# Top-k attention, a maxout MoE and a routed MoE: the planner also orders the transfers and gives out buffers as it places steps

## The chip, the cores and the metric

The kernel runs on one core of one Trainium2 chip. The metric is device time in microseconds from the first to the last instruction, as the median of several runs. TensorE (PE) multiplies, VectorE (DVE) does the top-k, ScalarE (ACT) copies out of PSUM and takes exponentials, GpSimd (POOL) does elementwise work between SBUF tiles, and SyncE (SP) issues the transfers.

## The reference, cut to what matters

```python
# q, k, v: (4 batches, 8 heads, 576 tokens, 64)
scores = q @ k.T / sqrt(64)
kth    = 32nd largest score of each row          # top_k = 32
attn   = softmax(where(scores >= kth, scores, -1e9))
x      = attn @ v                                # as (2304 tokens, 512)
h      = max(x @ w1, x @ w2, x @ w3)             # 512 x 768 each
x      = h @ w_out                               # 768 x 512
logits = x @ w_gate + modality_bias[modality_id] # 8 experts
e      = argmax(logits);  g = softmax(logits)[e]
out    = g * (relu(x @ e_w1[e]) @ e_w2[e])       # 512 x 1024, 1024 x 512
```

The weights of the first MoE come as 64-bit floats and are decoded on the chip. Products are made from a high and a low part of each operand (three matmuls instead of one).

## The kernel before, in words

The attention is cut into 72 units. A `full` unit is one query tile of 128 rows and one pair of heads; a `comb` unit joins the 64 rows that are left of a batch for two pairs. For each unit: `q_load` and `q_split` fetch a query tile and split it in high and low parts, `q_prep` transposes it; `scores` writes the scores to the PSUM tile `s` (one buffer, four banks, two key halves: half 1 first, then half 0), and `s_copy` copies each half to the SBUF tile `ss` (four buffers). Two folds on VectorE (L785) form the larger and the smaller of the two halves; a fold reads half 0 from PSUM and half 1 from `ss`. Eight rounds of `max` and `match_replace` on the folded rows give the threshold. Then `mask` and `expo` make the softmax numerators, `pt` transposes them, `av` multiplies by the values (PSUM tile `m`, two buffers), and `norm` and `x_split` write the input of the first MoE. Keys are loaded, split and transposed per pair of heads (`k_load`, `k_split`, `k_prep`), values per pair (`v_load`); `v_max` reads the values once more for a scale.

Three groups of query tiles per batch go through the first MoE (`moe1_steps`: three matmul chains per 128 columns, evacuated by ScalarE and VectorE, then `w_out`, transposes and gate). Its weights are decoded in 24 pieces during the first units (`weight_steps`). `route_early` computes the routing of the first three batches near unit 67: sums, ranks, and a table (L1416, TensorE, into a tile `m`). The last MoE groups run after the attention (`tail`), and then the experts.

The program names the steps slot by slot (one slot per unit, with positions between 0 and 1 inside it). `Plan.add` records for each step its engine, an estimated length, and the buffers that it reads and writes as (name, tenant, part, number of buffers). `Plan.run` then places steps by list scheduling: on the engine that is free first, the ready step with the smallest urgency, which is its number less the `soon` of the function that issued it (table `SOON`). A step waits for `data` (the end of other steps, plus a tail and a wake-up time) and for `order` (the other step has been placed). In `add` before, the first user of a tenant of a buffer name gets an `order` edge from the first user of the tenant named just before it, and in `run` every user of a tenant gets `data` edges from all users of the tenant that is as many back as there are buffers. Both follow the order in which the program names the tenants.

`tc.manual_schedule` keeps the order in which `run` calls the steps for PE, ACT, DVE and POOL. SP's queue is ordered by the framework's own scheduler. A transfer has a length of 60 to 540 ns in the plan and lands 2300 ns and a given extra time later.

Of the kernel before, what the change touches and what calls it, by code (L numbers as in the profile page):

```python
# [21 lines left out]
BIG = float(2.0 ** 100)  # L22
UP = float(2.0 ** 16)
# [3 lines left out]
class Plan:  # L27
# [16 lines left out]
    def add(self, engine, length, f, reads=(), writes=(), shared=False, lands=0):  # L44

        soon = self.soon
# [4 lines left out]
        data, order = set(), set()  # L51
        for places, w in ((reads, False), (writes, True)):
            for name, tenant, part, bufs in places:
                all_ = self.held.setdefault(name, {})
                if tenant not in all_:
                    if all_:
                        order.add(next(reversed(all_.values()))[0][0])
                    all_[tenant] = []
                uses = all_[tenant]
                if uses:  # L60
                    order.add(uses[0][0])
                data.update(m for m, q, v in uses if (w or v) and (q == part or q is None or part is None))
                uses.append((n, part, w))
                self.bufs[name] = bufs
        data.discard(n)
        order.discard(n)
        self.steps.append((engine, length, f, shared, data, order, lands, n - soon))

    def run(self):
        steps = self.steps  # L70
        for name, tenants in self.held.items():
            uses = [{n for n, _, _ in u} for u in tenants.values()]
            for old, now in zip(uses, uses[self.bufs[name]:]):
                for n in now:
                    steps[n][4].update(old)
        for n, s in enumerate(steps):
            s[4].discard(n)
            s[5].difference_update(s[4])
        after = [[] for _ in steps]
        left = [len(s[4]) + len(s[5]) for s in steps]  # L80
        for n, s in enumerate(steps):
            for m in s[4]:
                after[m].append((n, True))
            for m in s[5]:
                after[m].append((n, False))
        free = dict.fromkeys(self.WAKE, 0)
# [3 lines left out]
        locked = 0  # L90
        for n, s in enumerate(steps):
            if not left[n]:
                heapq.heappush(come[s[0]], (0, s[7], n))
        while True:
# [21 lines left out]
            end = t + length + self.TAIL[e] + lands  # L116
            for m, data in after[n]:
                to = steps[m][0]
                at = t if not data else t + length if e == to == "PE" else end + self.WAKE[to] + (self.SPARE if e != to else 0)
                ready[m] = max(ready[m], at)  # L120
                left[m] -= 1
                if not left[m]:
                    heapq.heappush(come[to], (ready[m], steps[m][7], m))
            f()
        assert not any(left)
# [4 lines left out]
def moe_chain_kernel(  # L130
# [52 lines left out]
    nc.sync.dma_start(wg, w_gate.rearrange("(c p) e -> p c e", p=128))  # L183
# [67 lines left out]
    nc.sync.dma_start(x2_dram[0:1, :], z)  # L251
# [40 lines left out]
    def whole(redo):  # L292
# [81 lines left out]
        def fetch(src, piece, signs=False):  # L374
# [6 lines left out]
            if wide:  # L381
                raw = rawf[:, k % 4 * 2 * PIECE:(k % 4) * 2 * PIECE + 2 * n * m].bitcast(I32)
                add("SP", 60, lambda: nc.sync.dma_start(raw.rearrange("p (c f) -> p c f", c=n), src.bitcast(I32)), (),
                    [at("raw", k, None, 1, k % 4)], lands=5 * n * m)
# [3 lines left out]
            add("SP", 60, lambda: nc.sync.dma_start(w.rearrange("p (c f) -> p c f", c=n), src), (), [at("wst", k, None, 1, k % 2)],  # L388
                lands=3 * n * m)
# [91 lines left out]

        def setup_bias():
# [7 lines left out]

            def f1():
                mod = box["mod"]
# [1256 lines left out]
```

## Time and profile before

| | |
|---|---|
| median of 3 runs | 1105.55 us (1104.78 to 1107.02) |
| profiled execution | 1103.24 us, span 1101.5 us |
| TensorE matmul | 944.6 us, 86% |
| VectorE | 769.1 us, 70% |
| ScalarE | 702.2 us, 64% |
| GpSimd | 560.6 us, 51% |
| mean granted TensorE clock | 0.929 of full |

Busy time is the time in which an engine executes an instruction; matmuls are pipelined and their ends are modelled. In a list in order of time, the brackets behind an instruction give the idle time of its engine just before it and what ended it. Stretches and starts are in microseconds from the span's start. Line numbers are those of the kernel before.

### The profile page before, as it was taken

To read this page: it belongs to the slowest core of one execution; us is meant where nothing else is said; L and a number is where in the kernel's file an instruction comes from. 1 tells how busy PE (TensorE), PEld (TensorE's weight loads), DVE (VectorE), ACT (ScalarE), POOL (GpSimd) and SP (SyncE) were. 2 spreads that over 40 slices of the span, in tenths; PEclk is the share of its full clock that TensorE was granted. 3 is DMA by queue.
4 is the path that set the end of the run, shared out by engine and by line. 5 is a ranking of instruction groups with operands and counts; after the bars stand their busy time and mean duration, and the time that the engine had idled before them with its cause. 6 is when DMAs were issued, how large, how long until landed. Compare 5 with 4: busy or idle time off the path is not lost. (4 is left out here: it accounts for less than half of the span.)

```text
span 1101.5 us, 22044 instructions
## 1 busy us (share of the span) xinstructions
PE 944.6 (86%) x7518; PEld 777.7 (71%) x7518; DVE 769.1 (70%) x2510; ACT 702.2 (64%) x1624; POOL 560.6 (51%) x831
## 2 busy tenths in 40 slices
PE   1546569999999899999999999974989989989995
PEld 0434448787778788777878778753779868868884
DVE  2799999989997969998887999996353511151110
ACT  1689898898877878887778887762453222342221
POOL 1578787576766666676566776662331111131010
PEclk9857689999999989999989999996989999999998
DMA  4652320224001113001011100000030331142000
GB/s 84 195 144 91 101 83 11 60 53 138 7 6 35 37 42 79 26 5 34 9 48 30 43 9 6 27 1 1 1 120 31 138 103 49 39 155 77 20 30 25
DMA packets 83795, 60.48 MB, mean 55 GB/s; under 512 B 67009, under 2 KB 67009, under 8 KB 83650
## 3 DMA queue, kind: packets, MB, share of 16 engines
q1 hardware_dynamic: 80770, 49.32, 15.8%
q0 software_dynamic: 2880, 9.44, 2.5%
q8 instruction: 65, 1.06, 0.4%
q14 instruction: 80, 0.66, 0.2%
HBM read 49.30 MB, written 9.44 MB: 53 GB/s over the span
## 5 line engine op out<-in xcount | busy, mean ns | idle before, releaser
L792 DVE MAX8 tk<-wk 128x8 f32<-128x288 f32 x576 | 235.9, 445 | 0.0
L847 POOL TENSOR_TENSOR ss<-mk,ss 128x576 f32<-128x576 bf16 x144 | 186.2, 1306 | 54.8 <-ACT mk L845 54.6
L803 DVE MATCH_REPLACE8 wk<-tk,wk 128x288 f32<-128x288 f32 x432 | 188.3, 441 | 0.0
L785 DVE TENSOR_TENSOR wk<-s,ss 128x576 f32<-128x576 f32 x144 | 106.9, 749 | 38.4 <-ACT ss L726 36.9
L845 ACT ACTIVATE mk<-ss,kb 128x576 bf16<-128x576 f32 x144 | 107.7, 773 | 33.7 <-POOL kb L741 33.5
L870 PE MATMUL t<-ident,ss 128*128 128x128 f32 x576 | 93.2, 297 | 34.2 <-ACT ss L853 31.5
L726 ACT ACTIVATE ss<-s 128x576 f32<-128x576 f32 x144 | 88.3, 647 | 50.6 <-PE s L715 49.1
L853 ACT ACTIVATE ss<-ss,kb 128x576 f32<-128x576 f32 x144 | 112.3, 782 | 6.4 <-POOL ss L847 6.1
L917 POOL TENSOR_SCALAR ss<-ss,r,nil 128x576 f32<-128x576 f32 x116 | 95.4, 828 | 30.5 <-DVE r L907 27.1
L1601 ACT ACTIVATE hid<-ph 128x512 f32<-128x512 f32 x36 | 21.5, 598 | 137.8 <-PE ph L1600 137.8
L715 PE MATMUL s<-ks,qt 128*128 128x288 f32 x512 | 96.1, 337 | 12.2 <-DVE wk L785 7.1
L870 PEld LDWEIGHTS t<-ident,ss 128*128 128x128 f32 x576 | 68.8, 151 | 47.3 <-ACT ss L853 37.1
L1625 POOL DMA_INDIRECT out_dram<-bo,tab x18 | 18.3, 1017 | 155.7 <-ACT bo L1624 148.4
L715 PEld LDWEIGHTS s<-ks,qt 128*128 128x128 f32 x512 | 80.9, 215 | 19.1 <-DVE wk L785 8.1
L1589 DVE TENSOR_TENSOR bxl<-px,bxh 128x512 fp32r<-128x512 f32 x18 | 12.4, 690 | 113.0 <-ACTq L1637 96.6
L874 ACT ACTIVATE pt<-t 128x512 f32<-128x512 f32 x144 | 84.3, 601 | 1.6 <-PE t L870 1.5
L938 PE MATMUL m<-pt,v 128*64 128x128 f32 x1024 | 75.7, 294 | 0.0
L938 PEld LDWEIGHTS m<-pt,v 128*64 128x64 f32 x1024 | 59.4, 145 | 11.9 <-issue 11.9
L1059 DVE SCALAR_TENSOR_TENSOR hb<-m,wfac,hb 128x320 f32<-128x320 f32 (+2 forms) x96 | 47.1, 491 | 19.5 <-PE m L1050 18.2
L1070 POOL TENSOR_TENSOR hl<-hb,hh 128x320 f16<-128x320 f32 (+2 forms) x54 | 36.9, 683 | 45.0 <-ACT hh L1065 44.9
L1600 PE MATMUL ph<-e1h,bxh 128*128 128x512 f32 x144 | 58.8, 408 | 1.2 <-ACT bxh L1588 0.7
L1621 PE MATMUL py<-e2h,bhh 128*128 128x512 f32 x144 | 58.0, 403 | 1.4 <-ACT bhh L1612 1.4
(312 smaller groups left out, 2734.3 us busy)
## 6 DMA issues: line engine op xcount, KB each, us to landing
raw<-in_moe_w_dram SPq DMA_DIRECT2D x6, 2048.0 KB, 9.7
raw<-in_moe_w_dram SPq DMA_DIRECT2D x18, 512.0 KB, 3.8
kraw<-in_v_dram SPq DMA_DIRECT2D x16, 288.0 KB, 2.8
kraw<-in_k_dram SPq DMA_DIRECT2D x32, 128.0 KB, 2.5
qraw<-in_q_dram SPq DMA_DIRECT2D x64, 64.0 KB, 1.9
v<-in_v_dram SPq DMA_DIRECT2D x32, 128.0 KB, 2.4
x_rows<-row SPq DMA_DIRECT2D x16, 256.0 KB, 2.0
raw<-in_moe_w_out_dram SPq DMA_DIRECT2D x6, 512.0 KB, 3.5
```

The lines of the kernel that those rows point to most:

```text
L715: PE.matmul(ST[u][:, hf, t, :HALF], qt[:, i, :], KS[bat(u), p][:, hd, k0:k0 + HALF], start=(n == 0), stop=(n == len(parts) - 1))
L726: A.activation(SS[u][:, :, hf * HALF:(hf + 1) * HALF], ST[u][:, hf, :, :HALF], AF.Copy)
L785: V.tensor_tensor(WK[u][:, :, w, :], ST[u][:, 0, :, :HALF], SS[u][:, :, HALF:S], op=op)
L792: V.max(TK[u][:, t, r * 8:r * 8 + 8], WK[u][:, t, 0, :])
L803: add("DVE", 426, lambda: V.match_replace(WK[u][:, t, 0, :], TK[u][:, t, r * 8:r * 8 + 8], WK[u][:, t, 0, :], NEG), [tk_at(u, (t, r))], [w ...
L845: A.activation(box["m"], SS[u][:, t, :], AF.Relu, bias=KTH[u][:, t, 1:2], scale=-BIG)
L847: add("POOL", 1250, lambda: G.tensor_tensor(SS[u][:, t, :], box["m"], SS[u][:, t, :], op=OP.subtract), [M], rows_at(u, t))
L853: A.activation(SS[u][:, t, :], SS[u][:, t, :], AF.Exp, bias=KTH[u][:, t, 0:1], scale=-scale * UP, accum_out=SUM[u][:, t:t + 1])
L870: PE.transpose(t[:, c, :], SS[u][:, i, c0:c0 + 128], ident)
L874: A.activation(o, box["t"], AF.Copy)
L917: add("POOL", 790, lambda: G.tensor_scalar(SS[u][:, t, :], SS[u][:, t, :], RR[u][:, t:t + 1], nil, op0=OP.mult, op1=OP.add), [at("r", u, N ...
L938: PE.matmul(ps[hd * 64:(hd + 1) * 64, 0, :], vt[:, c, hd, :], PT[u, hd][:, c, :], start=False, stop=(c == KC - 1), skip_group_check=True)
```

## The change

`Plan.add` no longer chains the tenants of a buffer in program order: it notes which step opens a tenant. `Plan.run` checks, when it is about to place such a step, which tenant had taken the buffer that comes free next. If that one has steps to come, the step is put aside until they are placed; if it ends later than now, the step comes back at that time; otherwise it takes the buffer. The order of the tenants is thus the order of placing.

SP is added to the engines whose order is kept. Each transfer is a step of its own, of 570 ns, that ends 2000 ns later plus its bytes at 180 per ns, with transfers in flight sharing that rate. The key, value and modality loads are split into single transfers; the gate weights and a zero row move from the head of the kernel to slot 2 (`late_loads`), the weight scales from slot -6 to -2. `k_prep` takes its buffer with the transposes instead of with the first copy. `s_copy` of half 0 moves from the slot before the unit's folds to position 0.13 of the unit's own slot, behind both folds, and the folds name both halves of `ss` as read. The table `SOON` is new. The diff, cut to its core:

```diff
-    TAIL = {"PE": 165, "ACT": 112, "DVE": 85, "POOL": 45, "SP": 2300}
-
-    SPARE = 0
+    TAIL = {"PE": 165, "ACT": 112, "DVE": 85, "POOL": 45, "SP": 2000}
+    RATE = 180.0
...
-    def add(self, engine, length, f, reads=(), writes=(), shared=False, lands=0):
...
-        data, order = set(), set()
+        data, order, opens, uses_ = set(), set(), [], []
         for places, w in ((reads, False), (writes, True)):
             for name, tenant, part, bufs in places:
-                all_ = self.held.setdefault(name, {})
-                if tenant not in all_:
-                    if all_:
-                        order.add(next(reversed(all_.values()))[0][0])
-                    all_[tenant] = []
-                uses = all_[tenant]
-                if uses:
+                uses = self.held.setdefault((name, tenant), [])
+                if not uses:
+                    opens.append((name, tenant))
+                elif uses[0][0] != n:
                     order.add(uses[0][0])
                 data.update(m for m, q, v in uses if (w or v) and (q == part or q is None or part is None))
                 uses.append((n, part, w))
+                if (name, tenant) not in uses_:
+                    uses_.append((name, tenant))
                 self.bufs[name] = bufs
         data.discard(n)
-        order.discard(n)
-        self.steps.append((engine, length, f, shared, data, order, lands, n - soon))
+        self.steps.append((engine, length, f, shared, data, order - data, size, n - self.soon, opens, uses_))
...
-        for name, tenants in self.held.items():
-            uses = [{n for n, _, _ in u} for u in tenants.values()]
-            for old, now in zip(uses, uses[self.bufs[name]:]):
-                for n in now:
-                    steps[n][4].update(old)
+        after, left, todo = [[] for _ in steps], [], {}
...
-            e = best[1]
+            now, e = best
             n = heapq.heappop(here[e])[1] if here[e] else heapq.heappop(come[e])[2]
-            _, length, f, shared, _, _, lands, _ = steps[n]
-            t = max(free[e], ready[n])
+            _, length, f, shared, _, _, size, _, opens, uses = steps[n]
+            late = 0
+            for x in opens:
+                had = taken.setdefault(x[0], [])
+                if len(had) >= self.bufs[x[0]]:
+                    old = had[-self.bufs[x[0]]]
+                    if todo[old]:
+                        wait.setdefault(old, []).append(n)
+                        late = None
+                        break
+                    late = max(late, max(t if d == e == "PE" else t + self.TAIL[d] + self.WAKE[e] for t, d in ends[old]))
+            if late is None:
+                continue
+            if late > now:
+                push(n, late)
+                continue
+            for x in opens:
+                taken[x[0]].append(x)
+            t = max(free[e], ready[n], now)
...
-            end = t + length + self.TAIL[e] + lands
+            end = t + length + self.TAIL[e]
+            if e == "SP":
+                end = max(end, pipe) + size / self.RATE
+                pipe = max(pipe, t + 1500) + size / self.RATE
...
+        def late_loads():
+            add("SP", ISSUE, lambda: nc.sync.dma_start(wg, w_gate.rearrange("(c p) e -> p c e", p=128)), (), [at("wg", 0)])
+            add("SP", ISSUE, lambda: nc.sync.dma_start(x2_dram[0:1, :], z), (), [at("rows", 0, "zero")])
...
+            m32 = modality.bitcast(I32).rearrange("(t two) -> t two", two=2)
+            for b in range(B):
+                add("SP", ISSUE, lambda b=b: nc.sync.dma_start(
+                    box["mod"][:, b, 1:NTT], m32[b * S:b * S + KC * 128, 0:1].rearrange("(c p) o -> p (c o)", p=128)),
+                    (), [at("bias", 0, b)], size=2048)
+                add("SP", ISSUE, lambda b=b: nc.sync.dma_start(box["mod"][:TL, b, 0:1], m32[b * S + KC * 128:(b + 1) * S, 0:1]),
+                    (), [at("bias", 0, b)], size=2048)
...
         def k_load(b, p):
-            def f():
-                raw = ap_.tile([128, NTT, 2, D], F32, name="kraw", bufs=2)
...
-            add("PE", 168, f, [at("kx", (b, p), (1, i)) for i in range(2)], [t])
+            add("PE", 168, f, [at("kx", (b, p), (1, i)) for i in range(2)], [t, ks_at(b, p, ("room", 2))])
...
         def v_load(b, p):
-            def f():
...
-                VT[b, p] = vt
-            add("SP", 300, f, (), [at("v", (b, p), None, 5)], lands=2000)
+            for i, hd in ((0, 0), (0, 1), (1, 0), (1, 1), (2, 1)):
+                def f(i=i, hd=hd):
+                    if (b, p) not in VT:
+                        VT[b, p] = ap_.tile([128, NTT, 2, D], F32, name="v", bufs=5)
+                    vt, src = VT[b, p], of_batch(v, b)[2 * p + hd]
...
+                add("SP", ISSUE, f, (), [at("v", (b, p), (i, hd), 5)], size=(131072, 16384, 16384)[i])
...
-                add("DVE", 664, f, [at("s", u, 0), ss_at(u, 0, 1), ss_at(u, 1, 1)], [wk_at(t, w) for t in range(2)])
+                add("DVE", 664, f, [at("s", u, 0)] + [ss_at(u, t, hf) for t in range(2) for hf in range(2)],
+                    [wk_at(t, w) for t in range(2)])
...
+        WSCALE = -2
         EARLY = 67
-        SOON = {"scores": 120, "s_copy": 120, "q_split": 120, "q_prep": 120, "k_split": 120, "k_prep": 120, "mm": -60, "ev": -30}
+        SOON = {"q_prep": 180, "prefetch_first": 180, "k_prep": 135, "k_split": 125, "scores": 120, "s_copy": 90,
+                "q_split": 90, "x_split": 55, "setup_bias": 45, "pt": 45, "f": 25, "av": 20, "recip": -5, "setup_routing": -5,
+                "k_load": -5, "mask": -5, "first_expert": -15, "v_max": -20, "norm": -25, "ev": -30, "weight_scales": -55,
+                "g": -60, "route_early": -70, "mm": -75, "scale_rows": -95, "v_load": -115}
...
-                sched(-6, weight_scales)
+                sched(WSCALE, weight_scales)
+                sched(2, late_loads)
...
+                if u0 is not None:
+                    put(0.13, s_copy, u0, 0)
...
                     put(0.36, scores, un, 0)
-                    put(0.42, s_copy, un, 0)
...
-            add("SP", 300, lambda: nc.sync.dma_start(raw1, e_w1[ds(e_value(first_e), 1)].rearrange("o (c p) f -> p (o c) f", p=128)),
-                [at("first", 0)], [at("raw", "first", None, 1, i) for i in range(4)], lands=12000)
+            add("SP", ISSUE, lambda: nc.sync.dma_start(raw1, e_w1[ds(e_value(first_e), 1)].rearrange("o (c p) f -> p (o c) f", p=128)),
+                [at("first", 0)], [at("raw", "first", None, 1, i) for i in range(4)], size=2097152)
...
-            with tc.manual_schedule(engines={E.PE, E.Activation, E.DVE, E.Pool}):
+            with tc.manual_schedule(engines={E.PE, E.Activation, E.DVE, E.Pool, E.SP}):
```

## Rows read from the trace of the kernel before

**Rows 1.** Busy time of an engine over the span (busy us, share, instructions), from the page.
```profile
PE 944.6 (86%) x7518; PEld 777.7 (71%) x7518; DVE 769.1 (70%) x2510; ACT 702.2 (64%) x1624; POOL 560.6 (51%) x831
```
**Rows 2.** Busy time by stage: stretch, length, busy us (instructions) per engine, PEclk, DMA, GB/s.
```profile
0.00:12.00 12.00, 0.75 (x4) 0.56 (x4) 3.96 (x17) 2.32 (x4) 3.13 (x14) 1.00 0.49 94
12.00:38.30 26.30, 7.03 (x35) 5.83 (x35) 7.22 (x37) 6.84 (x23) 3.79 (x8) 1.00 0.54 127
38.30:155.30 117.00, 68.68 (x436) 54.07 (x434) 115.86 (x352) 101.33 (x221) 91.52 (x110) 0.68 0.42 122
175.00:725.00 550.00, 526.54 (x4715) 436.32 (x4712) 495.81 (x1686) 453.08 (x1093) 366.40 (x585) 0.97 0.13 35
736.60:757.70 21.10, 0.58 (x6) 0.44 (x4) 20.23 (x85) 7.43 (x14) 8.51 (x13) 0.61 0.00 0
757.70:802.00 44.30, 43.15 (x376) 31.23 (x375) 13.75 (x47) 18.32 (x46) 11.33 (x18) 0.95 0.01 1
848.00:1101.50 253.50, 230.10 (x1113) 188.19 (x1113) 62.09 (x158) 69.86 (x125) 39.37 (x37) 0.97 0.21 71
```
**Rows 3.** SP in order of time: start us, us, engine, line, operation, out<-in, count.
```profile
0.76 0.46 SPq L183 DMA_DIRECT2D wg<-in_moe_w_gate_dram  x1
...
10.33 0.47 SPq L594 DMA_DIRECT2D v<-in_v_dram  x1
...
29.89 0.59 SPq L596 DMA_DIRECT2D v<-in_v_dram  x1
30.59 0.53 SPq L633 DMA_DIRECT2D qraw<-in_q_dram  x1
```
**Rows 4.** ScalarE in order of time, at the start; idle time and releaser in brackets.
```profile
13.23 0.81 ACT L547 ACTIVATE kx<-kraw 128x512 fp32r<-128x512 f32 x2
...
32.74 0.42 ACT L647 ACTIVATE qx<-qraw 128x256 fp32r<-128x256 f32 x1 [18.21 <-DMA qraw<-in_q_dram]
33.06 1.07 ACT L573 ACTIVATE ks<-t 128x512 fp32r<-128x512 f32 x2
```
**Rows 5.** TensorE in order of time, at the start.
```profile
14.66 1.26 PE L568 MATMUL t<-identr,kx 128*128 128x128 f32 x8 [0.15 <-DVE kx L551]
```
**Rows 6.** VectorE in order of time: the first fold.
```profile
38.28 0.76 DVE L785 TENSOR_TENSOR wk<-s,ss 128x576 f32<-128x576 f32 x1
```
**Rows 7.** TensorE in order of time, near the end of the attention.
```profile
736.58 0.60 PE L870 MATMUL t<-ident,ss 128*128 128x128 f32 x4
757.74 0.55 PE L1416 MATMUL m<-rhs,sel 128*128 128x15 bf16 x15 [20.57 <-DVE rhs L1411]
758.14 0.43 PE L1050 MATMUL m<-xh,w3h 128*128 128x320 f16 x1
...
761.43 0.56 PE L934 MATMUL m<-pt,v 64*64 64x128 f32 x4
```
**Rows 8.** VectorE in order of time: first folds of the last two units.
```profile
738.00 0.76 DVE L785 TENSOR_TENSOR wk<-s,ss 128x576 f32<-128x576 f32 x1 [0.51 <-ACT ss L726]
...
769.13 1.42 DVE L785 TENSOR_TENSOR wk<-s,ss 128x576 f32<-128x576 f32 x2 [1.65 <-ACT ss L726]
```
**Rows 9.** All engines in order of time: a second fold, the next scores, the next fold.
```profile
282.65 0.75 DVE L785 TENSOR_TENSOR wk<-s,ss 128x576 f32<-128x576 f32 x1
...
283.54 1.30 PE L715 MATMUL s<-ks,qt 128*128 128x288 f32 x8
...
290.81 0.75 DVE L785 TENSOR_TENSOR wk<-s,ss 128x576 f32<-128x576 f32 x1
```
**Rows 10.** Groups by line: busy us, mean ns; idle us before them, releasers.
```profile
L845 ACT ACTIVATE mk<-ss,kb 128x576 bf16<-128x576 f32 x144 | 107.7, 773 | 33.7 <-POOL kb L741 33.5
...
L726 ACT ACTIVATE ss<-s 128x576 f32<-128x576 f32 x144 | 88.3, 647 | 50.6 <-PE s L715 49.1 <-DVE wk L785 1.3
```
**Rows 11.** Transfers by line: count, KB each, median us from issue to landing.
```profile
kraw<-in_k_dram SPq DMA_DIRECT2D x32, 128.0 KB, 2.5
...
v<-in_v_dram SPq DMA_DIRECT2D x32, 128.0 KB, 2.4
```

More of the change, by code (lines that the diff above doesn't have):

```diff
@@ L22 @@
 BIG = float(2.0 ** 100)
+ISSUE = 570
 UP = float(2.0 ** 16)
@@ L42, in clear, with add @@
         self.steps, self.held, self.bufs = [], {}, {}
-    def add(self, engine, length, f, reads=(), writes=(), shared=False, lands=0):
-        soon = self.soon
+    def add(self, engine, length, f, reads=(), writes=(), shared=False, size=0):
         if not self.live:
@@ L89, in run, with push @@
         ready = [0] * len(steps)
-        locked = 0
-        for n, s in enumerate(steps):
+        taken, ends, wait = {}, {}, {}
+        locked, pipe, out = 0, 0, 0
+        def push(n, t):
+            heapq.heappush(come[steps[n][0]], (t, steps[n][7], n))
+        for n in range(len(steps)):
             if not left[n]:
-                heapq.heappush(come[s[0]], (0, s[7], n))
+                push(n, 0)
         while True:
@@ L115, in run @@
             free[e] = t + length
-            end = t + length + self.TAIL[e] + lands
+            end = t + length + self.TAIL[e]
+            if e == "SP":
+                end = max(end, pipe) + size / self.RATE
+                pipe = max(pipe, t + 1500) + size / self.RATE
+            f()
+            out += 1
             for m, data in after[n]:
                 to = steps[m][0]
-                at = t if not data else t + length if e == to == "PE" else end + self.WAKE[to] + (self.SPARE if e != to else 0)
+                at = t if not data else t + length if e == to == "PE" else end + self.WAKE[to]
                 ready[m] = max(ready[m], at)
@@ L122, in run @@
                 if not left[m]:
-                    heapq.heappush(come[to], (ready[m], steps[m][7], m))
-            f()
-        assert not any(left)
+                    push(m, ready[m])
+            for x in uses:
+                todo[x] -= 1
+                ends.setdefault(x, []).append((end - self.TAIL[e], e))
+                if not todo[x]:
+                    for m in wait.pop(x, ()):
+                        push(m, ready[m])
+        assert out == len(steps)
         self.clear()
@@ L565, in f @@
                     kx = KX2[b, p]
+                    if (b, p) not in KS:
+                        KS[b, p] = ap_.tile([128, 2, TL + S], F32R, name="ks", bufs=4)
                     box[hd] = psT.tile([128, 512], F32, name="t").bitcast(F32R)
@@ L570, in g @@
                 def g(hd=hd):
-                    if hd == 0:
-                        KS[b, p] = ap_.tile([128, 2, TL + S], F32R, name="ks", bufs=4)
                     A.activation(KS[b, p][:, hd, TL:S], box[hd], AF.Copy)
-                add("PE", 344, f, [at("kx", (b, p), (0, i)) for i in range(2)], [t])
+                add("PE", 344, f, [at("kx", (b, p), (0, i)) for i in range(2)], [t, ks_at(b, p, ("room", hd))])
                 add("ACT", 477, g, [t], [ks_at(b, p, hd)])
```

67 lines of the change are left out of this document (31 added, 36 removed).

## The prediction

> **What bounds the kernel now.** I read the busy shares first, then the busy time by stage, then, at the two stages with idle engines, the instructions in order of time. The shares [rows 1] name no single bound: TensorE is busy 86% of the span, VectorE 70%. The stages [rows 2] do. From 38.3 to 155.3 us VectorE is busy 115.86 of 117.00 us: the top-k and the decoding of the weights bound that stage, and TensorE idles in 48 us of it. From 175 to 725 TensorE is busy 526.54 of 550.00 us and VectorE 495.81: TensorE bounds, with VectorE not far behind. From 848 on, TensorE is busy 230.10 of 253.50 us in the experts, which are not planned by the code that changes. So the two long middle stages are full, and an ordering change finds little in them. What is not full are two short stretches: the first 38.3 us, in which VectorE works 3.96 + 7.22 = 11.18 us and idles 27.1, and 736.6 to 757.7, in which TensorE works 0.58 of 21.10 us.
>
> The first hole is one of transfer order. From 10.33 to 30.59 SP issues only values and modality ids: 25 of v and 9 of the ids, 34 issues in 20.26 us, 0.60 us each [rows 3]. The third query load stands behind them. ScalarE has the splitting of that query tile ahead of the copies of the first key tile in its queue, and waits 18.21 us for it, until 32.74; then it copies the keys (33.06), and the first fold of VectorE starts at 38.28 [rows 4, 6]. TensorE had the key transposes ready at 14.66 + 1.26 = 15.9 [rows 5].
>
> The second hole is one of buffer order. TensorE's next instruction at 736.6 is the routing table's matmul (L1416); it waits 20.57 us for VectorE, which is busy with that routing [rows 2, 7]. Right behind it stand matmuls of the first MoE that wait for nothing, and the value products of the last six units, of which the first runs at 761.43 [rows 7]. The old planner gives the two PSUM buffers "m" out in the order in which the program names them: every user of "m" that the program names after the table must wait until the table has had its own. The stall is thus in the plan itself. The last unit's fold comes at 769.13, 31 us after the one before, at 738.00 [rows 8].
>
> **The change, part by part.**
>
> *Transfers as planned steps.* SP joins the engines that keep the planner's order, and each transfer is a step of 570 ns (0.60 us measured) that ends after a latency and its size at 180 bytes per ns. Queries and keys keep their place; `v_load` gets -115 steps, so values go behind them; the modality ids are nine steps of their own. Nothing is added: the same transfers are issued. The first fold then needs one query load and four key loads: 0.76 + 5 x 0.60 = 3.8 us of issue, 2.5 to land [rows 3, 11], so keys are there at 6.3. From the splitting of the keys to the end of their transposes it took 13.23 to 15.92 = 2.7 us [rows 4, 5]; from the key copies to the fold 33.06 to 38.28 = 5.2 us [rows 4, 6]. Sum 6.3 + 2.7 + 5.2 = 14.2 us for the first fold, 24.1 us earlier. Not all of it is won, because VectorE is full afterwards: of the 11.18 us it did before the fold, some 5 (weight scales, bias) will be done after it. I take 24 - 5 = **19 us**. The ends: 24 if that work fits beside the keys' path; 10 if units 1 to 3, which each need a new key pair (four issues, 2.4 us, plus 2.5 to land, plus splitting), or the weights leave new gaps in VectorE's work. The stage behind it moves forward whole, because its bound is VectorE's work, which is the same, and the first MoE group starts relative to VectorE's eighth unit.
>
> The row says that an issue placed early held up what mattered. The Trainium skill says the opposite of what `v_load` now does (page "DMA: Bandwidth & Descriptors", section "Rules for kernel authors": issue a transfer early, compute, and wait for it late). By that rule the -115 makes values late, and the time would be that of the second rival, 1086; by the row it is the early issue that costs 18.21 us, and the time is the forecast.
>
> *Buffers handed out as steps are placed.* A step that opens a buffer now takes it when it is placed, and waits only for the tenant that had it before. So the table's matmul no longer stands ahead of ready work; besides, `route_early` gets -70 and sinks behind the last units' top-k. From 736.6 to 802 TensorE works 0.58 + 43.15 = 43.7 of 65.4 us [rows 2]; without the hole this work ends near 782, if VectorE lets it. VectorE works 20.23 + 13.75 = 34 us in the same stretch [rows 2], so it isn't the bound; what is late next is the last unit's chain, from its fold (at the earliest some 10 us after 738) through its top-k, softmax and value product. I take **20 us**, nearest to the stall's 20.57. The ends: 11 if VectorE still does all the routing first, so that the last fold moves only from 769 to 758; 21.7 if all idle time goes. The transfer of the first expert and the gate weights are off the path: `prefetch_first` loads long before the experts start, and the gate weights are used first when a MoE group ends.
>
> *Score copy behind the folds.* The fold reads half 0 from PSUM and half 1 from SBUF. Its copy of half 0 now comes after the folds instead of before, at 0.647 us each [rows 10]. VectorE loses a wait where that copy came ahead of the fold, but the one score buffer in PSUM is released later, by the copy plus what ScalarE has in front. In the unit shown the next scores start at 283.54, 0.14 us after the second fold ends (282.65 + 0.75) [rows 9]; so the scores do follow the folds, and the delay will move them. From the folds' end to the next fold at 290.81 VectorE has 7.4 us of other work [rows 9], against copy 0.65 + scores 1.30 + copy 0.65 = 2.6, so the next fold isn't late. TensorE waits only if nothing else is put ahead of the scores. I take **0**; the ends are -0.65 us and +1.42 us (a copy and a mask of 0.773 in front of it [rows 10]) for each unit; folds come every (769.13 - 38.28) / 71 = 10.3 us [rows 6, 8], so 550 / 10.3 = 53 units lie between 175 and 725.
>
> *New urgency table, weight scales at slot -2.* The same work in another order. In the middle stage TensorE's idle time is 550 - 526.5 = 23.5 us, so no more than that can be won there; a worse order can cost as much. I take 0.
>
> **Sum.** The profiled execution took 1103.24 us, 1.74 more than its span. 1103.24 - 19 - 20 = 1064.2. The median of the runs is 1105.55, 2.3 above; the same distance gives 1066.5. I forecast **1066 us**, 3.6% faster.
>
> **Rivals.**
>
> *Only the start* (chance 0.14). The table's matmul sinks, but another wait takes its place: the routing's last steps or the last unit's top-k, since VectorE is busy 20.23 of 21.10 us in the hole. For it: VectorE is full there. Against it: TensorE has 43 us of other work. 1105.5 - 19 = 1086.
>
> *Only the end: transfers come too late* (0.12). Place: the value products, which then wait for `v`. A value pair is five issues and 2.4 us to land, 5 x 0.60 + 2.4 = 5.4 us; were each of 16 pairs issued only when awaited, 86 us. The start would lose its 19 us as soon as four pairs come late. Against it: the planner's own latency of 2.0 us plus 131 KB at 180 bytes per ns, 2.7, is above the 2.4 measured [rows 11]. 1105.5 - 20 = 1086.
>
> *The middle gives too* (0.13). Free choice of PSUM buffers fills two thirds of TensorE's 23.5 us. 1066 - 16 = 1050.
>
> *Nothing* (0.05). What is won at the start is lost again in the full TensorE stage, for instance because the first MoE group waits for weights that are decoded later. 1105.
>
> *Slower: the score buffer becomes the loop* (0.10). Place: PSUM tile "s", of which there is one. With the copy behind the folds, TensorE's next scores wait for ScalarE, and as TensorE bounds this stage, its wait is lost time. Price: a copy of 0.65 and half a foreign instruction, 0.39, in 53 units = 55 us: 1066 + 55 = 1121. From 39 / 53 = 0.74 us in each unit on, nothing is left of the gain. For it: the scores follow the folds within 0.14 us in the unit shown. Against it: ready MoE matmuls can be put ahead of the scores, and TensorE has such work in nearly all of that stage.
>
> **How the numbers follow.** Forecast 0.46, with its own range 1056 to 1078 (10 to 24 us at the start, 11 to 21.7 at the end, and some us of the middle either way). Below 1046 lies about 0.05 (part of the third rival), above 1097 the last two, 0.15. The range of 8 in 10 is **1046 to 1097**. A measurement of this kernel tells 0.2%, 2 us, from no change. Faster: 0.46 + 0.14 + 0.12 + 0.13 = 0.85; same 0.05; slower 0.10.
>
> **What would show it.** Right: the first fold starts at 12 to 18 us, not 38.28; no query load stands behind values on SP; VectorE's idle time before 40 us falls from 27 to under 12; the table's matmul waits for under 3 us and the last two folds are some 10 us apart, not 31; scores, after the folds, are preceded by other TensorE work. Wrong: TensorE idle between 175 and 725 well above 23.5 us with scores waiting for the copy (the slower rival); value products that wait for a transfer (the second rival); a new TensorE wait of 10 us or more in the last 60 us before the tail; a middle stage of other length than 550 us for the same work.

## The result and the profile after

The kernel after the change takes **1035.46 us** (median of 4 runs, 1031.39 to 1036.44) where the one before, timed beside it, takes 1105.4. The ratio is 0.9358, with a 95% interval of 0.9331 to 0.9385: 6.4% faster. I had forecast 1066 us and a range of 1046 to 1097; the time lies 11 us below the range. The direction was right and the amount was wrong.

The profiled run after took 1031.39 us, with a span of 1029.5 against 1101.5: 72.0 us less. It is the quickest of the four runs, with a mean granted clock of 0.974 where the others had 0.936 to 0.945, so the readings of the clock below are those of one run. First the row of the page that answers to [rows 1], busy time and number of instructions of each engine:

```profile
PE 921.5 (90%) x7518; PEld 765.3 (74%) x7518; DVE 777.4 (76%) x2510; ACT 699.8 (68%) x1624; POOL 556.5 (54%) x831
```

All counts are as before: the same work was done. Yet TensorE's busy time fell from 944.6 to 921.5 us, by 23.1, and its idle time from 1101.5 - 944.6 = 156.9 to 1029.5 - 921.5 = 108.0, by 48.9; together 72.0. That busy time can fall with the same instructions is what my forecast did not reckon with.

To see where the time went I cut both spans at the same work rather than at the same microseconds: at the first folds of units 0, 10, 70 and 71. Stretch, its length, then busy us (instructions) of PE, PEld (TensorE's loading of weights), DVE, ACT and POOL, PEclk (the granted share of TensorE's clock), DMA share, GB/s. Before:

```profile
38.30:155.70 117.40, 69.08 (x440) 54.39 (x439) 116.25 (x354) 101.72 (x222) 91.62 (x110) 0.68 0.42 123
155.70:738.00 582.30, 552.90 (x4928) 456.98 (x4925) 526.70 (x1784) 476.54 (x1146) 390.14 (x617) 0.97 0.13 34
738.00:769.10 31.10, 11.36 (x95) 8.13 (x96) 21.93 (x90) 10.69 (x23) 10.68 (x14) 0.67 0.00 1
769.10:1101.50 332.40, 303.51 (x2025) 251.84 (x2022) 93.07 (x231) 104.12 (x209) 61.23 (x69) 0.97 0.19 65
```

After:

```profile
11.40:140.40 129.00, 75.10 (x520) 59.95 (x519) 128.11 (x398) 105.85 (x237) 89.62 (x112) 0.89 0.48 135
140.40:679.60 539.20, 527.81 (x4831) 440.90 (x4832) 528.16 (x1770) 471.78 (x1141) 388.06 (x619) 0.99 0.14 37
679.60:690.70 11.10, 11.10 (x105) 8.78 (x104) 11.10 (x40) 8.01 (x20) 6.70 (x11) 1.00 0.00 0
690.70:1029.50 338.80, 301.99 (x2038) 250.69 (x2036) 106.23 (x292) 107.72 (x215) 67.02 (x76) 0.97 0.19 64
```

- **Start.** The first fold comes at 11.4 instead of 38.3 us, 26.9 earlier; the stretch to unit 10 is 11.6 longer, since VectorE does 398 instructions in it instead of 354 and is busy in all but 0.9 us. Left at unit 10: 15.3 us.
- **Middle**, units 10 to 70: 582.3 to 539.2, **43.1 us**, three fifths of the whole.
- **End**, units 70 to 71: 31.1 to 11.1, 20.0 us.
- **Behind the last fold**: 332.4 to 338.8, 6.4 us lost. VectorE has 292 instructions there instead of 231: routing that was done ahead of the last fold is now done behind it. TensorE has a new wait there, of 6.38 us at 742.70, for a copy by ScalarE (L1159) that stands behind the splitting of an expert's weights. It is as long as the loss, but run 9 below takes 341.6 us here without it and run 12 336.9 us with one of 6.32, so the cause of the loss is open.

Sum: -15.3 - 43.1 - 20.0 + 6.4 = -72.0.

The start, in order of time. SyncE (start, us, engine, line, operation) issues one query load, the keys of two pairs of heads (four issues each), two query loads and the keys of a third pair. The fourth query load is issued at 13.37 us, ahead of all values (the first at 17.95). Before, it stood behind 34 other issues until 30.59 [rows 3]:

```profile
0.75 0.46 SPq L666 DMA_DIRECT2D qraw<-in_q_dram  x1
1.27 1.01 SPq L560 DMA_DIRECT2D kraw<-in_k_dram  x2
2.32 1.20 SPq L562 DMA_DIRECT2D kraw<-in_k_dram  x2
3.56 1.14 SPq L560 DMA_DIRECT2D kraw<-in_k_dram  x2
4.74 1.16 SPq L562 DMA_DIRECT2D kraw<-in_k_dram  x2
5.94 1.10 SPq L666 DMA_DIRECT2D qraw<-in_q_dram  x2
7.17 0.94 SPq L560 DMA_DIRECT2D kraw<-in_k_dram  x2
...
13.37 0.59 SPq L666 DMA_DIRECT2D qraw<-in_q_dram  x1
```

ScalarE copies the keys at once, at 6.73 us, not at 33.06 behind a wait of 18.21 [rows 4]; and VectorE's first fold follows [rows 6]:

```profile
6.73 1.10 ACT L603 ACTIVATE ks<-t 128x512 fp32r<-128x512 f32 x2 [0.89 <-PE t L600]
...
10.68 0.65 ACT L759 ACTIVATE ss<-s 128x576 f32<-128x576 f32 x1 [1.37 <-PE s L748]
```

```profile
11.37 1.42 DVE L818 TENSOR_TENSOR wk<-s,ss 128x576 f32<-128x576 f32 x2 [5.21 <-ACT ss L759]
```

The end: folds of the last two units [rows 8], and the routing table's matmul, which now comes 22 us after the last fold and waits 2.58 us instead of 20.57 [rows 7]:

```profile
679.60 1.42 DVE L818 TENSOR_TENSOR wk<-s,ss 128x576 f32<-128x576 f32 x2
...
690.74 0.74 DVE L818 TENSOR_TENSOR wk<-s,ss 128x576 f32<-128x576 f32 x1
```

```profile
713.19 0.54 PE L1456 MATMUL m<-rhs,sel 128*128 128x15 bf16 x15 [2.58 <-DVE scratch L1551]
```

**The middle.** Most units took 8 to 10 us in both kernels. The kernel before had two groups of slow ones (units 28 to 35 and 47 to 52), most of them 10 to 17.6 us. TensorE's idle time in the middle fell by 18.0 us (29.4 to 11.4). Its busy time fell by 25.1, for two reasons that can be read.

First, the granted clock. I read the middle in stretches of 3 us. Before, TensorE ran at half clock, 0.50, for 37.6 us of it (shares of a stretch weighed in); after, for 6.8. (Run 12 below, with 0.938 in the mean, has 9.4 us of half clock in its middle, so the small figure does not come from the higher mean clock of this run.) One such place in the kernel before, with the stretch ahead of it, in which the clock falls, and matmuls in it:

```profile
380.70:383.70 3.00, 0.87 (x6) 0.70 (x6) 3.00 (x11) 3.00 (x9) 1.57 (x3) 0.86 0.35 83
383.70:386.70 3.00, 2.05 (x11) 1.64 (x11) 3.00 (x12) 3.00 (x8) 1.87 (x2) 0.50 0.53 136
386.70:389.70 3.00, 3.00 (x14) 2.56 (x13) 1.17 (x6) 2.05 (x7) 0.62 (x3) 0.50 0.38 86
```

```profile
386.29 2.29 PE L715 MATMUL s<-ks,qt 128*128 128x288 f32 x8
```

The scores' eight matmuls take 2.29 us here, and 1.30 in [rows 9]. The last stretch counts as 3.00 us busy of 3.00, and up to half of that is the clock. At most 37.6 - 6.8 = 30.8, halved, 15.4 us of busy time went that way.

Second, 97 matmuls fewer lie in it (4928 to 4831). 72 are the weight checks of three matrices: before at 184.1 to 195.8 us, after at 110.1 to 131.6, ahead of unit 10, where TensorE has idle time. Durations in ns (min/median/max), first and last start. Before:

```profile
L454 PE MATMUL m<-w1h x24: 219/219/229, 184.1 to 185.3; 128*128 128x128 f16 x24
...
L454 PE MATMUL m<-w3h x24: 219/219/230, 194.5 to 195.8; 128*128 128x128 f16 x24
```

After:

```profile
L475 PE MATMUL m<-w1h x24: 219/219/229, 110.1 to 111.4; 128*128 128x128 f16 x24
...
L475 PE MATMUL m<-w3h x24: 311/311/311, 129.1 to 131.6; 128*128 128x128 f16 x24
```

Three times some 1.4 us, so 4 us. That leaves 25.1 - 15.4 - 4 = some 6 us of busy time that I have not assigned; 25 other matmuls, net, moved too.

### The profile page after: what moved, and what is told of

Same layout as the page of the kernel before. It is cut to its first block, busy times and chain, and to the rows that moved or that the text cites. A ratio compares the mean times of both kernels' runs of the same rounds, so it can differ in the third digit from the quotient of the medians.

```text
span 1029.5 us, 21977 instructions
## 1 busy us (share of the span) xinstructions
PE 921.5 (90%) x7518; PEld 765.3 (74%) x7518; DVE 777.4 (76%) x2510; ACT 699.8 (68%) x1624; POOL 556.5 (54%) x831
## 5 line engine op out<-in xcount | busy, mean ns | idle before, releaser
L879 ACT ACTIVATE mk<-ss,kb 128x576 bf16<-128x576 f32 x144 | 109.8, 777 | 12.6 <-POOL kb L774 12.2
L759 ACT ACTIVATE ss<-s 128x576 f32<-128x576 f32 x144 | 93.5, 649 | 33.6 <-PE s L748 22.0
L748 PE MATMUL s<-ks,qt 128*128 128x288 f32 x512 | 94.2, 329 | 14.2 <-ACT ss L759 13.3
L951 POOL TENSOR_SCALAR ss<-ss,r,nil 128x576 f32<-128x576 f32 x116 | 94.9, 823 | 18.4 <-DVE r L941 11.5
L904 PE MATMUL t<-ident,ss 128*128 128x128 f32 x576 | 87.6, 285 | 17.2 <-ACT ss L887 14.9
L1629 DVE TENSOR_TENSOR bxl<-px,bxh 128x512 fp32r<-128x512 f32 x18 | 12.4, 690 | 111.7 <-ACTq L1677 94.9
L748 PEld LDWEIGHTS s<-ks,qt 128*128 128x128 f32 x512 | 78.1, 207 | 20.6 <-ACT ss L759 17.6
L904 PEld LDWEIGHTS t<-ident,ss 128*128 128x128 f32 x576 | 66.4, 146 | 27.4 <-ACT ss L887 17.7
L972 PEld LDWEIGHTS m<-pt,v 128*64 128x64 f32 x1024 | 58.0, 143 | 11.8 <-issue 11.4
L833 DVE MAX8 zk<-wk 128x8 f32<-128x288 f32 x144 | 59.7, 442 | 0.0
L1084 PE MATMUL m<-xh,w1h 128*128 128x320 f16 (+2 forms) x192 | 53.5, 283 | 6.9 <-ACT row L1159 6.4
```

Of the source, the lines that this page charges most:

```text
L748: PE.matmul(ST[u][:, hf, t, :HALF], qt[:, i, :], KS[bat(u), p][:, hd, k0:k0 + HALF], start=(n == 0), stop=(n == len(parts) - 1))
L759: A.activation(SS[u][:, :, hf * HALF:(hf + 1) * HALF], ST[u][:, hf, :, :HALF], AF.Copy)
L879: A.activation(box["m"], SS[u][:, t, :], AF.Relu, bias=KTH[u][:, t, 1:2], scale=-BIG)
L904: PE.transpose(t[:, c, :], SS[u][:, i, c0:c0 + 128], ident)
L951: add("POOL", 790, lambda: G.tensor_scalar(SS[u][:, t, :], SS[u][:, t, :], RR[u][:, t:t + 1], nil, op0=OP.mult, op1=OP.add), [at("r", u, N ...
L972: PE.matmul(ps[hd * 64:(hd + 1) * 64, 0, :], vt[:, c, hd, :], PT[u, hd][:, c, :], start=False, stop=(c == KC - 1), skip_group_check=True)
```

## The experiments

Twelve further kernels were measured. Theory A says that the handing out of buffers as steps are placed gave the middle; B, the score copy behind the folds; C, the urgency table. The times are medians; the ratios are to the kernel before, on the same chip. Cut at the same folds, by the profiled run of each (us). (The new slot of the weight scales, the late loads and the split into single transfers have no run of their own.)

| kernel | time | first fold | to unit 10 | units 10 to 70 | 70 to 71 | then |
|---|---|---|---|---|---|---|
| before | 1105.4 | 38.3 | 117.4 | 582.3 | 31.1 | 332.4 |
| after | 1035.5 | 11.4 | 129.0 | 539.2 | 11.1 | 338.8 |
| 1 all tiles in program order | 1096.3 | 11.2 | 133.3 | 582.7 | 32.8 | 333.9 |
| 2 SyncE's order not kept | 1039.0 | 11.5 | 129.1 | 542.0 | 11.1 | 342.2 |
| 3 copy ahead of the folds | 1043.3 | 12.1 | 131.5 | 544.5 | 11.0 | 342.7 |
| 4 old urgency table | 1065.7 | 11.9 | 130.0 | 571.1 | 14.0 | 338.4 |
| 5 only "m" in program order | 1069.1 | 11.5 | 130.0 | 559.4 | 29.7 | 335.4 |
| 6 all but "m" in program order | 1053.7 | 11.3 | 133.1 | 553.1 | 12.6 | 341.5 |
| 7 before, issues at 570 ns | 1108.9 | 15.5 | 128.8 | 593.0 | 32.1 | 336.6 |
| 8 = 1 and 4 | 1093.0 | 12.2 | 131.7 | 585.5 | 28.7 | 333.1 |
| 9 as 5, slow tenants free | 1051.1 | 11.3 | 129.2 | 554.9 | 14.1 | 341.6 |
| 10 transfers at the old price | 1049.9 | 14.2 | 139.8 | 542.1 | 11.1 | 340.6 |
| 11 MoE at -45 | 1041.7 | 11.3 | 130.3 | 546.5 | 12.4 | 339.7 |
| 12 MoE at -85 | 1033.5 | 11.2 | 131.0 | 539.8 | 12.4 | 336.9 |

**1. All tiles in program order.** In the changed kernel, each tile's tenants are chained as before:

```
+                    line = self.line.setdefault(name, [])
+                    if line and line[-1][0][0] != n:
+                        order.add(line[-1][0][0])
+                    line.append(uses)
...
+            for old, now in zip(line, line[self.bufs[name]:]):
+                for n in now:
+                    steps[n][4].update(old - {n})
```

> The changed kernel with one part undone: the tenants of a buffer are again chained in the order in which the program names them. Transfers, score copy and urgency table stay as changed. Theory A (the middle stage gained because buffers are handed out as steps are placed): both the 43 us of the middle and the 20 us at the end go, about 1035 + 45 to 63 = 1080 to 1098 us; TensorE again spends over 25 us at half clock between the 11th and the 71st unit. Theory B (the score copy behind the folds) and theory C (the urgency table): only the 20 us at the end go, about 1055 us.

Measured: 1096.27 us, ratio 0.9937 (0.9916 to 0.9959). The middle and the stall at the end are both back in full, with the new table, the new transfers and the new score copy all in place:

```profile
144.50:727.20 582.70, 547.42 (x4930) 450.98 (x4931) 534.31 (x1774) 479.58 (x1146) 388.61 (x621) 0.97 0.13 35
727.20:760.00 32.80, 12.18 (x98) 9.03 (x97) 23.03 (x99) 11.13 (x24) 11.10 (x16) 0.64 0.00 0
```

So A holds: without it, nothing of the 63 us of middle and end is won.

**2. SyncE's order not kept by hand.**

```
-            with tc.manual_schedule(engines={E.PE, E.Activation, E.DVE, E.Pool, E.SP}):
+            with tc.manual_schedule(engines={E.PE, E.Activation, E.DVE, E.Pool}):
```

> The changed kernel, but SP's queue is again left to the framework's scheduler; the other four engines keep their order word for word. If the order of the transfers is what moved the first fold from 38 to 11 us, the first fold comes 15 to 25 us late again and the time is 1050 to 1060 us; if the split into single transfers alone did it, the time stays at 1035 us.

Measured: 1038.95 us, ratio 0.9392 (0.9351 to 0.9434), first fold at 11.5. The expectation of a lost start fell. Keeping SyncE's order is worth 3.5 us by the medians, and the two intervals overlap, so it can't be told from nothing.

**3. The copy of half 0 ahead of the folds again** (with the fold's reads as before).

```
-                if u0 is not None:
-                    put(0.13, s_copy, u0, 0)
...
+                    put(0.42, s_copy, un, 0)
```

> The changed kernel with the score copy of half 0 back in the slot before, ahead of the folds, and the folds naming half 1 alone. Theory B: the middle gives back most of its 43 us, 1065 to 1080 us, with VectorE waiting some 35 us for ScalarE's score copies as before (6.6 us after). Theories A and C: 1035 to 1043 us.

Measured: 1043.26 us, ratio 0.9438 (0.9423 to 0.9454): the copy's new place is worth some 8 us. Between 140 and 690 us, VectorE's fold waits for ScalarE's copies (line waited for, us in total, times, longest) in this kernel, and after:

```profile
DVE wk L818 <- ACT ss L759: 7.1, 10, 1.1
```

```profile
DVE wk L818 <- ACT ss L759: 1.3, 1, 1.3
```

**4. The old urgency table.**

```
-        SOON = {"q_prep": 180, "prefetch_first": 180, "k_prep": 135, "k_split": 125, "scores": 120, "s_copy": 90,
...
+        SOON = {"scores": 120, "s_copy": 120, "q_split": 120, "q_prep": 120, "k_split": 120, "k_prep": 120, "mm": -60, "ev": -30}
```

> The changed kernel with the old urgency table (8 entries, values not deferred, routing not sunk). Theory C: 1065 to 1080 us. Theories A and B: the start and the end lose a little, 1037 to 1050 us.

Measured: 1065.71 us, ratio 0.9643 (0.9625 to 0.966). The table is worth 30 us here, nearly all of it in the middle, which takes 31.9 us longer than after:

```profile
141.90:713.00 571.10, 542.52 (x4940) 453.09 (x4941) 539.93 (x1802) 479.56 (x1149) 391.78 (x624) 0.97 0.14 35
```

So C holds as well as A: with the buffers free but the old table, most of the middle isn't won. The end (14.0) and what follows (338.4) are within 3 us of the kernel after. The first fold stays at 11.9: holding back the values by -115 is not what moved it.

**5 and 6. Which tile.** The chain of run 1 for one tile name alone, the PSUM tile "m" with its two buffers; and for all other tiles:

```
-                    line = self.line.setdefault(name, [])
+                    line = self.line.setdefault(name, []) if name == "m" else []
```

```
+                    line = self.line.setdefault(name, []) if name != "m" else []
```

> The changed kernel, but the tenants of one tile name alone, the PSUM tile m with its two buffers, are chained in the order of the program again; every other tile is handed out as steps are placed. Theory M (the order of m alone cost the middle and the end): as with all tiles chained, 1088 to 1098 us, the folds of units 10 and 70 at least 575 us apart, those of units 70 and 71 over 25 us apart, and some 440 matmuls between the folds of units 0 and 10, not 520. Rival N (many tiles each cost a little): 1040 to 1065 us, units 10 to 70 in 545 to 560 us.

> The other way round: every tile is chained in program order again except the PSUM tile m. Theory M: as the changed kernel, 1031 to 1046 us, units 10 to 70 in 538 to 546 us, and 10 to 13 us between the last two folds. Rival N: 1060 to 1090 us, units 10 to 70 over 560 us.

Measured: 1069.09 (ratio 0.967, 0.9625 to 0.9714) and 1053.68 (0.9521, 0.9491 to 0.9551). Neither theory is right as it stood. "m" alone brings back the whole stall at the end (29.7 us between the last folds; 12.6 with all others chained) and 20 us of the middle; the other tiles together 14 us of the middle. The two make 34 of the 43.5 us that run 1 brings back, so 9 or 10 us come back only when both are chained. TensorE's wait at the routing table's matmul is 17.31 us in run 5 and 2.92 in run 6. Of "m" alone, the stretch to unit 10 and the end:

```profile
11.50:141.50 130.00, 70.26 (x443) 54.89 (x442) 128.78 (x394) 104.23 (x232) 88.36 (x111) 0.88 0.49 134
...
700.90:730.60 29.70, 11.84 (x101) 8.61 (x99) 22.91 (x101) 10.91 (x24) 11.85 (x17) 0.71 0.00 0
```

and of all but "m" the stretch to unit 10:

```profile
11.30:144.40 133.10, 75.28 (x516) 58.75 (x515) 131.93 (x398) 105.61 (x232) 91.77 (x113) 0.68 0.47 130
```

443 matmuls before unit 10 with "m" in program order, 516 with "m" free (520 after): it is "m" that lets the weight checks move forward. The same three matrices are checked at 170.0 to 180.6 us in run 5 and at 109.4 to 132.2 in run 6.

**7. The kernel before with the new price of an issue**, and nothing else: the length of each transfer step is 570 ns for each issue in it.

```
-                add("SP", 60, f, (), [at("qraw", (b, j, p), None, 3)])
+                add("SP", 570, f, (), [at("qraw", (b, j, p), None, 3)])
...
-            add("SP", 300, f, (), [at("v", (b, p), None, 5)], lands=2000)
+            add("SP", 2850, f, (), [at("v", (b, p), None, 5)], lands=2000)
```

> The kernel before, with one thing changed: the planner's length of a transfer step, 570 ns for each issue in it (570 for one, 2280 for the keys' four, 2850 for the values' five, 5130 for the nine of the modality ids) in place of 60 to 540. Theory I (the planner's price of an issue made the hole at the start): the first fold starts at 12 to 20 us, not at 38.28, and the time falls by 8 to 20 us, to 1085 to 1097. Rival (SyncE's order must be kept by hand, or the values made less urgent): first fold over 30 us, 1102 to 1107 us.

Measured: 1108.89 us, ratio 1.0031 (1.0007 to 1.0055). Half of theory I holds: the first fold comes at 15.5, so in this kernel the wrong price did make the hole. The other half fell: no time is won. Unit 10 is 11.4 us earlier than before (144.3 to 155.7), and then units 10 to 70 take 593.0 us, 10.7 more:

```profile
144.30:737.30 593.00, 560.36 (x4964) 461.03 (x4962) 532.66 (x1789) 478.61 (x1152) 392.12 (x622) 0.96 0.13 34
```

TensorE runs 52.0 us of this at half clock, against 37.6 before; half of the difference is 7.2 us, and its busy time is 7.5 us longer, with 36 more matmuls in it. The start won here was given back in the middle: my rival "nothing", for the start. Program order alone is not the reason. Runs 1 and 8 keep it, their unit 10 comes 11.2 and 11.8 us earlier than before, their middles take 582.7 and 585.5 us, and they end 8 and 12 us ahead of the kernel before. Why the middle of run 7 grew is not shown.

**8. Program order and the old table together.**

> The changed kernel with both undone: all tiles chained in program order and the old urgency table. Undone alone, the first cost 61 us (1096.3) and the second 30 us (1065.7). If the two are worth their own sums, 1096.3 + 30.3 = 1127 us (1115 to 1132). Rival: the table can only choose among steps that are free to move, so with the chain it is worth nothing and the time is that of the chain alone, 1090 to 1100 us, units 10 to 70 in 575 to 590 us.

Measured: 1093.04 us, ratio 0.9889 (0.9866 to 0.9912). The rival holds: the parts don't add up. With free buffers the table is worth 30 us; with tenants in program order it is worth nothing, or some 3 to 5 us less than nothing. In the middle, free buffers with the old table win 14.4 us (585.5 in this run, 571.1 in run 4), and the new table on top of them 31.9.

**9. As run 5, with the slow tenants of "m" free**: the bounds' matmuls, the first expert's, the routing's sums and table.

```
-            i, a, b = new(), at("m", new(), None, 2), at("m", new(), None, 2)
+            i, a, b = new(), at("m", ("slow", new()), None, 2), at("m", ("slow", new()), None, 2)
...
+                    line = self.line.setdefault(name, []) if name == "m" and not (isinstance(tenant, tuple) and tenant[0] == "slow") else []
```

> As the run with the tile m alone in program order (1069.1 us), but the tenants that wait for a chain on VectorE (the two matmuls of each scale bound, the first expert's, the routing's sums and its table) are taken out of that chain; MoE matmuls, value products and weight checks stay in it. Theory S (a few slow tenants hold the two buffers for all that the program names after them): the last two folds are 10 to 13 us apart, units 10 to 70 take 538 to 546 us, and the time is 1033 to 1046 us. Rival E (only the end stall is theirs; in the middle it is MoE matmuls and value products that wait for each other's turn): the end stall goes, units 10 to 70 stay at 553 to 562 us, 1048 to 1058 us.

Measured: 1051.07 us, ratio 0.9496 (0.9468 to 0.9524). Rival E: the end stall goes (29.7 to 14.1 us), and the middle stays long, at 554.9, with its 4928 matmuls and 433 before unit 10:

```profile
11.30:140.50 129.20, 72.69 (x433) 55.81 (x434) 128.28 (x394) 105.55 (x236) 90.23 (x112) 0.62 0.48 135
140.50:695.40 554.90, 537.42 (x4928) 447.05 (x4925) 529.81 (x1773) 472.76 (x1142) 389.98 (x619) 0.99 0.14 36
```

The table's matmul waits 1.45 us, where it waited 17.31 in run 5: the end was the table's tenancy, as I had said, though the run frees it together with other slow tenants. In the middle what is left in the chain, MoE matmuls, value products and weight checks, waited for each other's turn; these were not freed one by one.

**10. Transfers at the old price** in the changed kernel, with values not held back (`ISSUE = 60`, no `v_load` in the table).

> The changed kernel with the planner's price of an issue at 60 ns instead of 570 and with the value loads at urgency 0 instead of -115, so that values are issued from the start. Theory T (the transfers' order is worth little: VectorE's work before unit 10 is what it is, and a start won is given back there): 1034 to 1046 us, the fold of unit 10 at 139 to 146 us, wherever the first fold comes. Rival (the start was worth its 15 us): the first fold after 20 us, unit 10 after 150 us, 1048 to 1060 us.

Measured: 1049.88 us, ratio 0.9498 (0.9469 to 0.9527). The rival's amount holds, at another place than it said: the first fold is at 14.2, but unit 10 comes at 154.0, because units 2 and 3 are late (46.9 and 64.6 us, against 40.8 and 51.0 after). A query load again stands behind values on SyncE, ScalarE waits for it, and VectorE for weights:

```profile
30.11 0.42 ACT L680 ACTIVATE qx<-qraw 128x256 fp32r<-128x256 f32 x1 [9.50 <-DMA qraw<-in_q_dram]
```

```profile
35.04 0.43 DVE L374 TENSOR_SCALAR scratch<-raw 128x512 int32<-128x512 int32 x1 [6.79 <-DMA raw<-in_moe_w_dram]
```

The middle stays at 542.1, so here a start that is lost reaches the end.

**11 and 12. MoE matmuls sooner or later** (`"mm": -45` and `"mm": -85` instead of -75).

> The changed kernel with the first MoE's matmuls at urgency -45 instead of -75. If TensorE's idle time before unit 10 (129.0 - 75.1 = 53.9 us) can be filled by naming these matmuls sooner: more than 520 matmuls there, and 1020 to 1031 us. Rival: VectorE, busy 128 of those 129 us, sets what is ready; nothing is pulled forward, and matmuls put ahead of scores delay the folds: 1034 to 1050 us.

> The changed kernel with the first MoE's matmuls at urgency -85 instead of -75, the other direction from the run at -45, which took 1041.7 us. If the slope goes on (6.2 us for 30 steps, matmuls ahead of scores delaying the folds), 1030 to 1035 us, at best a version faster than both kernels by some 2 us. Rival: the matmuls then come too late, TensorE has more of them left behind the last fold: 1036 to 1050 us, and more than 339 us from the last fold to the end.

Measured: 1041.72 (ratio 0.942, 0.9392 to 0.9448) and 1033.52 (0.935, 0.933 to 0.9371). Sooner pulls nothing forward (514 matmuls before unit 10) and costs 6 us. Later is 2 us below the changed kernel's median, with overlapping intervals: not told apart, so no version that beats it was found. For -95 there is no measurement.

## Why the prediction was wrong, step by step

**What failed: the middle.** The step was "In the middle stage TensorE's idle time is 550 - 526.5 = 23.5 us, so no more than that can be won there", with the value 0. 43.1 us were won. The idle time was the smaller part (18.0 us). The step took two things as fixed that aren't: that busy time is work (up to 15.4 us of it was half clock, which stood in [rows 2] as PEclk 0.97, and I did not read it), and that the matmuls of a stage stay in it (the weight checks went to the stage ahead, in which I had myself noted 48 us of idle TensorE). Of my signs of being wrong, the last one came: a middle of other length for the same work. The value 0 failed because I priced *buffers handed out as steps are placed* at the one stall that the trace showed plainly, the routing table's, and the urgency table by itself, as reordering. Run 1 shows that with all buffers in program order none of the 43 us is there, runs 5 and 6 that 20 us hang on "m" and 14 on the other tiles; runs 4 and 8, that free buffers alone win 14.4 us of the middle, and that the new table, worth nothing without them, wins 31.9 on top. The Trainium skill's page "Perfetto Trace Analysis" (section "Identifying the Most-Contended Engine") says that the busy share of matmuls is not a good measure of how close a kernel is to the roofline (the chip's peak), because pipelined matmuls look smaller in a trace; this trace agrees with the warning, by another cause, the clock: 944.6 and 921.5 us for the same 7518 matmuls. My rival "the middle gives too" had the place, but "two thirds of TensorE's 23.5 us" was bound by the same cap, and so the range ended at 1046.

**Start: 19 us forecast, 15.3 measured.** The mechanism was right: values ahead of a query load (the fourth; I had called it the third), 18.21 us of wait. The first fold came 2.8 us earlier than my 14.2. VectorE's displaced work was 7.4 us, not 5 (of 11.19 us ahead of the fold 3.79 are left), and up to unit 10 it works another 4.5 us more than before. I ascribed the gain to `v_load` at -115 and SyncE's order. Runs 2 and 4 show that neither is needed for the first fold (11.5 and 11.9 us). Run 7 shows that in the kernel before the price of an issue in the plan is enough to move it, to 15.5. In run 10 it comes at 14.2 with neither the new price nor -115, so more than one part of the change removes the hole; which one does so there is not shown. Units 2 and 3, late in run 10, are not late in run 4 (37.4 and 50.9 us), where the price is new and values are not held back. That the gain would reach the end was a guess: it did in the kernel after and mostly in runs 1 and 8, and it did not in run 7.

By the rule of the Trainium skill's page "DMA: Bandwidth & Descriptors" (section "Rules for kernel authors"), to issue early, values held back would have come late. The trace after does not agree: no value product waits for a transfer. Run 10, which issues values early, pays 9.50 us on a query load.

**End: 20 us forecast, 20.0 measured.** The stall was the table's tenancy of "m" (runs 5 and 9), free buffers remove most of it without `route_early` at -70 (run 4: 14.0 us), and the last folds are 11.1 us apart, as I had said ("some 10"). Not foreseen: 6.4 us given back behind the last fold. VectorE now does 13 us of work there that it did ahead of it; that this is the cause is not shown.

**Score copy: 0 forecast, some 8 us measured** (run 3), a gain, of 0.1 us a unit, within the ends I gave. The reason was in my text, the fold's wait for the copy; the slower rival, that the scores would wait, did not come: in the middle they wait 1.9 us in all for ScalarE.

Put together: the two terms that I counted, measured, would have made a time of 1103.24 - 15.3 - 20.0 = 1067.9. Each came within 4 us, and what I valued at nothing was the larger half.

## What to carry to other kernels

An engine's busy time is no floor for a stage: read the granted clock beside it, and ask which of its instructions could run in another stage where the engine idles. When one rule of a planner is lifted (here: buffers in program order), one plainly visible stall is a sample of what the rule costs, not the whole; and what a priority table is worth depends on how much is free to move. Time won in one place need not arrive at the end: some 11 us won by unit 10 reached it for the most part in runs 1 and 8 and were given back in run 7.

## What the runs showed that I had not expected

Idle time may cost TensorE twice, because half clock goes with it. Run 1 differs from the kernel after in program order alone: in its middle TensorE is idle for 35.3 us, and runs 29.3 us at half clock, against 11.4 and 6.8 after. All fourteen kernels fit: where TensorE idles for 11.1 to 13.4 us of the middle, it runs 6.8 to 12.5 us at half clock; for 17.5 to 19.7, 14.1 to 17.9; for 27.0 to 35.3, 29.3 to 54.1. Ahead of the fall shown above it worked 0.87 of 3.00 us. That the idle time brings the fall is read from this order; no run changes one without the other. One line shows both levels, 2.4 and 1.2 GHz: the checks' matmuls take 219 ns each at 110.1 to 111.4 us and 311 at 129.1 to 131.6, 24 of them 1.3 and 2.5 us. The two stretches (PEclk is the third figure from the end):

```profile
110.10:111.40 1.30, 1.30 (x26) 1.30 (x25) 1.30 (x8) 1.30 (x4) 0.67 (x2) 1.00 0.71 180
129.10:131.60 2.50, 2.50 (x26) 2.47 (x24) 2.50 (x8) 1.83 (x5) 1.11 (x5) 0.50 0.28 110
```

In the middle of the kernel after, TensorE is busy 527.81 of 539.20 us and VectorE 528.16: both are full, which fits that shifting the MoE's urgency either way (runs 11 and 12) won nothing that can be told.
